# Seven products instead of eight in the second channel product too, in the wide chunks of a spectral filter with a token and channel MLP

## The chip, the cores and the metric

One Trainium2 chip, one of its cores. The metric is device time in microseconds of one execution. TensorE (PE) does the matrix products, with its weight loads (PEld) shown apart; VectorE (DVE), ScalarE (ACT) and GpSimd (POOL) do elementwise work; SyncE (SP) issues most transfers. Matrix results lie in PSUM, in eight banks of 128 x 512 f32; everything else is in SBUF.

## The reference, cut to what matters

```python
X = np.fft.rfft(x, axis=1)                       # x: (8, 3008, 256)
Yr = Xr @ w_r - Xi @ w_i + b_r                   # the same for Yi; both soft-thresholded
x = np.fft.irfft(Y, n=3008, axis=1)
h = np.maximum(xt @ w_tok1, 0.0) @ w_tok2        # xt: x with tokens last; d_tok = 256
u = x + h.transpose(0, 2, 1)
h2 = np.maximum(u @ w_ch1, 0.0) @ w_ch2          # 256 -> 1536 -> 256 channels
return u + h2
```

The change lies in the last product, `@ w_ch2`, for the batches 2 to 7.

## The kernel before, in words

The kernel first works through the spectra (TensorE, with VectorE, ScalarE and GpSimd beside it), interleaved with the channel MLP of batches 0 and 1. From 1133 us on, the channel MLP of batches 2 to 7 runs alone: this is `channel7`, the stage that the change rewrites. Its tokens come in 18 wide chunks, six for each pair of batches: one of 896 tokens, then five of 1024. `uf` holds a chunk's u: 128 channels on the partitions, two channel blocks t, tokens along the row. The hidden layer has 12 blocks of 128, taken as six pairs p; one chunk and one pair is called a step here (108 steps).

Every product is done to float32 accuracy in three matmuls (`mm3`, lines 196 to 198): operands are split into a rounded high part and a remainder, the low part, and high x high, high x low and low x high are summed in PSUM.

In a step, u is a 2 x 2 block matrix (two channel blocks by two halves of the tokens), and so is the pair's part of w_ch1. `first7` (L1018) does this product in Strassen's form (Winograd's variant): seven products of 128 x 128 by 128 x 512 in place of eight. The seven operands of u are made once a chunk (`sum_u` L991, `split_u7` L1004), those of the weights once for the kernel (`weigh`, during the last narrow chunk), and the four results are put together from PSUM and from copies of PSUM (`sn`) by ScalarE and VectorE; `rectify` (L1029) then makes the high part (ScalarE, L1032) and the low part (VectorE, L1033) of each of the four rectified blocks. `second7` (L1061) multiplies these blocks with w_ch2 as plain blocks: eight products a step, into four PSUM banks (`pos`) that collect over the six pairs. It runs one step behind `first7`. At the end of a chunk `finish7` adds u and stores.

Between the steps `make_u` (L841) makes the u of a coming chunk, one group of 376 or 470 tokens at a time: its matmuls are the `pu` rows of the profile, and its results are copied to `uf` by ScalarE (L867).

The order of the work: each engine runs its own queue in order. The order in a queue is not the order of the Python text alone: at build time a scheduler emits instructions by priority (text order) among those that it holds for ready. So what stands on each engine is read from the built kernel.

## Time and profile before

| | us |
|---|---|
| three timed runs | 2397.62, 2397.76, 2399.40; median 2397.76 |
| profiled execution, own time | 2399.55 |
| its span | 2397.8 |
| the stage of the wide chunks | from 1133.1 to the end |
| PE, DVE, ACT, POOL busy over the span | 98%, 59%, 48%, 11% |

POOL works only ahead of 1134 us; in the stage of the wide chunks it does nothing. The profile counts a matmul as busy from its start until its result has landed, and matmuls overlap; what one costs in a dense queue is the distance between two starts.

### The profile page before, as it was taken

The page shows a single profiled execution, that of the slowest core. Times are in us where ns is not written, and L with a number is a line of the kernel's source. Part 1 is how long each engine was busy: PE and PEld are TensorE (multiplying, and loading weights), DVE is VectorE, ACT ScalarE, POOL GpSimd, SP SyncE. Part 2 cuts the span into 40 slices and gives each one's busy share as a digit, 9 for nine tenths or more (in the row PEclk, how much of TensorE's full clock was granted, in tenths as well). Part 3 has the DMA queues.
Part 4 walks back from the last instruction along what each step waited for, and adds up shares of the span by engine and source line. Part 5 has one row for each costly group of instructions (what it writes and reads, how often), then busy time and mean ns, then how long its engine had stood idle before and what let it go on. Part 6 is the DMA issues. An engine that isn't in the chain of part 4 may idle for free.

```text
span 2397.8 us, 32249 instructions
## 1 busy us (share of the span) xinstructions
PE 2360.6 (98%) x12524; PEld 2063.7 (86%) x12524; DVE 1417.6 (59%) x2220; ACT 1143.3 (48%) x2033; POOL 252.7 (11%) x223
## 2 busy tenths in 40 slices
PE   8999999999999999999999999999999999999999
PEld 7778899999988888898988888898888889888887
DVE  7966766655646564555555555555555555555554
ACT  6754445544434443433444444444444444444543
POOL 0000332232323322330000000000000000000000
PEclk9999999999999999999999999999999999999999
DMA  8765467655555545433213112122311112222100
GB/s 217 237 222 158 152 205 241 198 167 181 176 181 169 185 149 171 141 128 126 64 60 91 57 49 61 37 81 60 91 57 38 52 57 82 60 86 60 40 1 36
DMA packets 149766, 277.06 MB, mean 116 GB/s; under 512 B 10933, under 2 KB 94477, under 8 KB 149613
## 3 DMA queue, kind: packets, MB, share of 16 engines
q1 hardware_dynamic: 115225, 208.40, 29.5%
q10 hardware_dynamic: 34388, 66.60, 8.2%
q8 instruction: 99, 1.62, 0.3%
q14 instruction: 54, 0.44, 0.1%
HBM read 177.57 MB, written 97.39 MB: 115 GB/s over the span
## 4 chain that ended last, share of the span: by engine, by line
PE 87%; DVE 5%; DMA 3%; ACT 1%; issue 1%; POOL 1%; SPq 1%; ACTq 0%; DVEq 0%; POOLq 0%
PE po L196 10%; PE po L197 10%; PE po L198 10%; PE pu L860 5%; PE sx L196 3%; PE sx L197 3%; PE sx L198 3%; PE px L482 2%; PE ph L196 2%; PE ph L197 2%; PE ph L198 2%; PE sw L196 2%; PE pm L198 2%; PE sw L197 2%; PE sw L198 2%; PE pm L196 2%
## 5 line engine op out<-in xcount | busy, mean ns | idle before, releaser
L196 PE MATMUL po<-hh,w2h 128*128 128x512 f32 (+3 forms) x1176 | 453.4, 386 | 1.2 <-DVE o L965 0.9
L197 PE MATMUL po<-hlo,w2h 128*128 128x512 f32 (+3 forms) x1176 | 449.3, 382 | 1.1 <-DVE hlo L899 1.1
L198 PE MATMUL po<-hh,w2l 128*128 128x512 f32 (+3 forms) x1176 | 449.1, 382 | 0.0
L1032 ACT ACTIVATE hh<-sn 128x512 fp32r<-128x512 f32 (+1 forms) x432 | 270.7, 627 | 86.5 <-DVE sn L1052 56.8
L1033 DVE SCALAR_TENSOR_TENSOR hlo<-sn,hh 128x512 fp32r<-128x512 f32 (+1 forms) x432 | 291.0, 674 | 10.0 <-ACT hh L1032 0.6
L197 PEld LDWEIGHTS po<-hlo,w2h 128*128 128x128 f32 x1176 | 221.2, 188 | 38.3 <-DVE hlo L899 2.2
L196 PEld LDWEIGHTS po<-hh,w2h 128*128 128x128 f32 x1176 | 221.2, 188 | 38.1 <-ACT xf L484 1.0
L198 PEld LDWEIGHTS po<-hh,w2l 128*128 128x128 f32 x1176 | 221.0, 188 | 38.0
L1041 DVE TENSOR_TENSOR sn<-sq,sn 128x512 f32<-128x512 f32 (+1 forms) x108 | 73.4, 680 | 290.1 <-PE sq L198 266.8
L1037 ACT COPY sn<-sx 128x512 f32<-128x512 f32 (+1 forms) x108 | 62.5, 579 | 341.4 <-PE sx L198 341.3
L149 DVE TENSOR_TENSOR xtl<-xf,xth 128x768 fp32r<-128x768 f32 x84 | 85.1, 1013 | 117.9 <-ACT xth L146 117.8
L196 PE MATMUL pm<-wmh,xth 128*128 128x256 f32 x504 | 146.2, 291 | 4.8 <-ACT xth L146 3.0
L899 DVE SCALAR_TENSOR_TENSOR hlo<-ph,hh 128x512 fp32r<-128x512 f32 (+3 forms) x156 | 98.7, 636 | 82.6 <-ACT hh L898 82.1
L867 ACT COPY uf<-pu 128x470 f32<-128x470 f32 (+15 forms) x152 | 60.5, 425 | 178.3 <-PE pu L860 177.5
L198 PE MATMUL pm<-wmh,xtl 128*128 128x256 f32 x504 | 142.6, 285 | 0.8 <-DVE xtl L149 0.8
L197 PE MATMUL pm<-wml,xth 128*128 128x256 f32 x504 | 142.4, 283 | 0.0
L860 PEld LDWEIGHTS pu<-g,b 96*128 96x128 f32 x1024 | 133.1, 194 | 3.5
L898 ACT ACTIVATE hh<-ph 128x512 fp32r<-128x512 f32 (+3 forms) x156 | 86.4, 556 | 103.1 <-PE ph L198 91.9
L860 PE MATMUL pu<-g,b 96*128 96x94 f32 x1024 | 131.3, 274 | 0.0
L149 POOL TENSOR_TENSOR yl<-z,yh 128x512 fp32r<-128x512 f32 x72 | 95.9, 1332 | 274.2 <-ACT yh L146 268.1
L196 PE MATMUL ph<-uh,w 128*128 128x512 f32 (+3 forms) x312 | 118.9, 382 | 3.6 <-DVE hlo L899 2.7
L197 PE MATMUL ph<-ul,w 128*128 128x512 f32 (+3 forms) x312 | 116.2, 373 | 0.0
(185 smaller groups left out, 5223.6 us busy)
## 6 DMA issues: line engine op xcount, KB each, us to landing
wt<-wt_d SPq DMA_DIRECT2D x28, 940.0 KB, 5.8
x<-in_x SPq DMA_DIRECT2D x39, 480.0 KB, 4.9
wt<-ws_d SPq DMA_DIRECT2D x36, 512.0 KB, 4.3
a<-a_d SPq DMA_DIRECT2D x36, 512.0 KB, 5.5
b_d<-bt ACTq DMA_DIRECT2D x36, 512.0 KB, 5.5
a_d<-a ACTq DMA_DIRECT2D x36, 480.0 KB, 4.0
wt<-wt_d SPq DMA_DIRECT2D x21, 752.0 KB, 5.2
b<-b_d SPq DMA_DIRECT2D x32, 480.0 KB, 6.5
```

The source lines that it names most:

```text
L149: lo_eng.tensor_tensor(out=lo, in0=src, in1=hi.bitcast(F32), op=ALU.subtract)
L196: PE.matmul(out, lhsT=wh, rhs=xh, start=start, stop=False, skip_group_check=more)
L197: PE.matmul(out, lhsT=wh, rhs=xl, start=False, stop=False, skip_group_check=more)
L198: PE.matmul(out, lhsT=wl, rhs=xh, start=False, stop=stop, skip_group_check=more)
L860: PE.matmul(pt[:, s * TOKS:(s + 1) * TOKS], lhsT=b2[:, s, cs], rhs=g2[:, 0 if s0 + s == 0 else 1], start=False, stop=s == k - 1)
L867: S.copy(out=ufs[m][:, ct, lo - at:hi - at], in_=pt[:, lo - c0:hi - c0])
L898: S.activation(out=hh, in_=pt, func=AF.Relu)
L899: V.scalar_tensor_tensor(out=hlo, in0=pt, scalar=0.0, in1=hh.bitcast(F32), op0=ALU.max, op1=ALU.subtract)
L1032: S.activation(out=hh, in_=t, func=AF.Relu)
L1033: V.scalar_tensor_tensor(out=hlo, in0=t, scalar=0.0, in1=hh.bitcast(F32), op0=ALU.max, op1=ALU.subtract)
L1037: S.copy(out=snap[0], in_=x)
L1041: V.tensor_tensor(out=snap[0], in0=q, in1=snap[0], op=ALU.add)
```

## The change

The second product gets the same seven-product scheme. The rectified block matrix (two hidden blocks by two token halves) is now what u is for the first product, and the pair's part of w_ch2 takes the role of the weights. New in the code:

- `weigh2` makes the weight operands of w_ch2, during the last narrow chunk beside `weigh`. Three operands of each set are kept apart (`ws`, `ws2`), and the fourth is written over the weight block that is no longer needed.
- `begin_pair` gives a step seven operands `op` (high and low side by side) in nine buffers; `high` makes the high parts on ScalarE. `lower` makes five low parts on GpSimd (b22, t1, t2, t4, t3), `above` two on VectorE (b11, b21).
- `step` writes a step of both products as one sequence: `one(new, i)` are the seven products of w_ch1 for the new step, `two(old, i)` the seven of w_ch2 for the step before. `snap` copies a PSUM bank to SBUF on ScalarE. t1, t2, t4 are sums on VectorE, t3 is one on GpSimd.
- Of the seven second products, five collect in PSUM over the six pairs (`total`); the products 3 and 4 each belong to one quarter of the output and are added to `uf` in every step (`taken`, VectorE). At a chunk's end the sums of the totals are added to `uf`: seven additions on VectorE, two on GpSimd.
- `first_u` and `rest_u` make the seven operands of u (seven splits and four sums a chunk, as before), with smaller buffers. `make_u` in this stage uses the banks x and y of the step in place of a bank of its own, and comes behind a step that `when` picks.

The diff, with weights and buffers that only change place left out:

```diff
 def make_u(g):
-            pt = bank("pu")
+            pt = wc["banks"]["xy"[ct]] if "banks" in wc else bank("pu")
...
+    def weigh2(q):
...
+        V.tensor_tensor(out=a.rearrange("m p t i c -> m (p t i c)"), in0=h.rearrange("m f c -> m (f c)").bitcast(F32), in1=l.rearrange("m f c -> m (f c)").bitcast(F32), op=ALU.add)
...
+        split(ws[:, :, :, 0], ws[:, :, :, 1], sf[:, :, :3], S, V)
+        split(h[:, 0::2, 128:], l[:, 0::2, 128:], s4, S, V)
...
+    FIRST = {1: ("x", "b11"), 2: ("y", "b21"), 3: ("w", "b22"), 4: ("x", "t4"), 5: ("w", "t1"), 6: ("x", "t2"), 7: ("x", "t3")}
+    SECOND = {1: "b11", 2: "b21", 3: "b22", 4: "t4", 5: "t1", 6: "t2", 7: "t3"}
...
     def channel7(ns):
...
+        total = {1: pair[0][:, 0], 5: pair[0][:, 1], 6: pair[1][:, 0], 7: pair[1][:, 1], 2: bank("po")}
+        banks = wc["banks"] = {k: bank("s" + k) for k in ("x", "w", "y")}
...
+        def begin_pair(n, p):
+            h = chunks[n][2] // 2
+            ops = {k: tail.tile([128, 2, CW], F32R, tag="op", name="op", bufs=9)[:, :, :h] for k in ("b11", "b22", "t1", "b21", "t2", "t4", "t3")}
+            return n, p, h, ops, {}
...
+        def above(out, in0, in1, op):
+            V.scalar_tensor_tensor(out=out, in0=in0, scalar=0.0, in1=in1, op0=MAX, op1=op)
...
+        def high(new, k, src=None):
+            S.activation(out=new[3][k][:, 0], in_=new[4][k] if src is None else src, func=AF.Relu if k in ("b11", "b21") else AF.Copy)
+
+        def lower(new, k, eng=G):
+            add(new[3][k][:, 1], new[4][k], new[3][k][:, 0].bitcast(F32), eng, SUB)
+
+        def taken(old, i, q):
+            out = quarters(old[0])[q]
+            add(out, banks["y"][:, :old[2]], out)
+
+        def step(new, old, last=False):
...
+            if new:
+                one(new, 1)
+                v["b11"] = snap(new, "x")
+                one(new, 5)
+                v["b22"] = snap(new, "w")
+            if old:
+                two(old, 1)
...
+            if new:
+                one(new, 6)
+                v["x2"] = snap(new, "x")
+                one(new, 2)
+                add(v["b11"], b["y"][:, :h], v["b11"])
+                high(new, "b11")
+                one(new, 3)
+                add(v["x2"], b["w"][:, :h], v["x2"])
+                S.activation(out=v["x2"], in_=v["x2"], func=AF.Relu)
+                one(new, 7)
+                add(v["b22"], b["x"][:, :h], v["b22"])
+                S.activation(out=v["b22"], in_=v["b22"], func=AF.Relu)
+                high(new, "b22")
+            if old:
+                two(old, 3)
+                taken(old, 3, 1)
+            if new:
+                sums(new, "t1", "t2", "t4", "t3")
+                above(v["t1"], v["b11"], v["x2"], SUB)
+                add(v["t2"], v["b22"], v["t1"])
+                high(new, "t1")
+            if old:
+                two(old, 5)
+            if new:
+                one(new, 4)
+                high(new, "b21", b["x"][:, :h])
+                above(v["t4"], b["x"][:, :h], v["t2"], SUB)
+                above(new[3]["b21"][:, 1], b["x"][:, :h], new[3]["b21"][:, 0].bitcast(F32), SUB)
+                high(new, "t2")
+                high(new, "t4")
+                lower(new, "t1")
+                add(v["t3"], v["b22"], v["x2"], G, SUB)
+                above(new[3]["b11"][:, 1], v["b11"], new[3]["b11"][:, 0].bitcast(F32), SUB)
+                high(new, "t3")
+                for k in ("b22", "t2", "t4", "t3"):
+                    lower(new, k)
...
+            if old:
+                two(old, 2)
...
+                two(old, 6)
...
+                two(old, 4)
+                taken(old, 4, 2)
+                two(old, 7)
+                if ends:
+                    add(fin, L[7], fin)
+                    for t in (u21, u22):
+                        add(t, fin, t, V if last else G)
+                    store(old[0])
...
+            for p in range(half):
+                new = begin_pair(n, p)
+                step(new, old)
+                old = new
+                if n < ns[-1] and p == half - 2:
+                    first_u(n + 1)
+                if n < ns[-1] and p == half - 1:
+                    rest_u(n + 1)
+                if (n, p) in when:
+                    make_u(when[n, p])
+                    load_group(when[n, p] + 1)
+        step(None, old, True)
```

The built order shows what this puts on the engines in a step. ScalarE before, one step of two 512-token halves: `sn` are the copies from PSUM (L1037, L1039, L1043, L1049), `hh7` the four high parts.

```order
L1037 COPY sn_15515<-sx_15511 128x512 [waits PE_49]
L1039 COPY sn_15516<-sw_15512 128x512 [waits PE_49]
L1043 COPY sn_15517<-sx_15511 128x512 [waits PE_49,Activation_49]
L1032 ACTIVATE hh7_15535<-sn_15515 128x512 [waits DVE_49]
L1049 COPY sn_15518<-sz_15514 128x512 [waits PE_49,Activation_49]
L1032 ACTIVATE hh7_15543<-sn_15517 128x512 [waits DVE_49]
L1032 ACTIVATE hh7_15556<-sn_15518 128x512 [waits DVE_49]
L1032 ACTIVATE hh7_15560<-sn_15516 128x512 [waits DVE_49]
```

Eight instructions, and none waits for GpSimd. The same engine now, from the second copy of bank x in a step to the first copy of the next step: `sn_17093` is x2, `sn_17085` b22, and `op_17070` to `op_17076` are, by number, the operands b11, b22, t1, b21, t2, t4, t3; the `ts` are the sums t1, t2, t4, t3.

```order
L1108 COPY sn_17093<-sx_10834 128x512 [waits PE_49]
L1112 ACTIVATE op_17070<-sn_17080 128x512 [waits DVE_49]
L1147 ACTIVATE sn_17093<-sn_17093 128x512 [waits DVE_49]
L1150 ACTIVATE sn_17085<-sn_17085 128x512 [waits DVE_49]
L1112 ACTIVATE op_17071<-sn_17085 128x512 [waits Activation_49]
L1112 ACTIVATE op_17072<-ts_17115 128x512 [waits DVE_49]
L1112 ACTIVATE op_17073<-sx_10834 128x512 [waits PE_49]
L1112 ACTIVATE op_17074<-ts_17116 128x512 [waits DVE_49]
L1112 ACTIVATE op_17075<-ts_17117 128x512 [waits DVE_49]
L1112 ACTIVATE op_17076<-ts_17118 128x512 [waits Pool_49]
L1108 COPY sn_17164<-sx_10834 128x512 [waits PE_49]
```

The step has twelve instructions on this engine in place of eight; the high part of t3 waits for GpSimd, and the next step's first copy of bank x stands behind it in the queue.

GpSimd, which had nothing in this stage, at the end of one chunk and in the first step after it: the two `uf` rows are the chunk's closing additions, `op_17071` is the low part of b22, `op_17072` that of t1, `ts_17118` is the sum t3.

```order
L1101 TENSOR_TENSOR uf_15484<-t_16992,uf_15484 128x512 [waits DMAHW2_49,DMAHW1_49,DVE_49]
L1101 TENSOR_TENSOR uf_15484<-t_16992,uf_15484 128x512
L1101 TENSOR_TENSOR op_17071<-sn_17085,op_17071 128x512 [waits PE_49,Activation_49]
L1101 TENSOR_TENSOR op_17072<-ts_17115,op_17072 128x512 [waits PE_49,Activation_49]
L1101 TENSOR_TENSOR ts_17118<-sn_17085,sn_17093 128x512 [waits Pool_49]
L1101 TENSOR_TENSOR op_17074<-ts_17116,op_17074 128x512 [waits PE_49,Activation_49]
L1101 TENSOR_TENSOR op_17075<-ts_17117,op_17075 128x512 [waits PE_49,Activation_49]
L1101 TENSOR_TENSOR op_17076<-ts_17118,op_17076 128x512 [waits PE_49,Activation_49]
```

Six instructions a step have moved here or are new; the sum t3 is third, behind the low parts of b22 and t1.

VectorE now, one step, from the sum b11 to the low part of b21: `sn<-sy`, `sn<-sw` and `sn<-sx` are the sums b11, x2 and b22, `op_17154` and `op_17157` the low parts of b11 and b21, `uf` the two `taken`, `ts_17199`, `ts_17200` and `ts_17201` are t1, t2 and t4.

```order
L1101 TENSOR_TENSOR sn_17164<-sy_10836,sn_17164 128x512 [waits Activation_49]
L1104 SCALAR_TENSOR_TENSOR op_17154<-sn_17164,op_17154 128x512 [waits Activation_49]
L1101 TENSOR_TENSOR sn_17177<-sw_10835,sn_17177 128x512 [waits PE_49,Activation_49,Pool_49]
L1101 TENSOR_TENSOR sn_17169<-sx_10834,sn_17169 128x512 [waits PE_49]
L1101 TENSOR_TENSOR uf_16115<-sy_10836,uf_16115 128x512 [waits PE_49]
L1104 SCALAR_TENSOR_TENSOR ts_17199<-sn_17164,sn_17177 128x512 [waits Activation_49]
L1101 TENSOR_TENSOR ts_17200<-sn_17169,ts_17199 128x512 [waits DVE_49,Activation_49,Pool_49]
L1101 TENSOR_TENSOR uf_16115<-sy_10836,uf_16115 128x512 [waits PE_49]
L1104 SCALAR_TENSOR_TENSOR ts_17201<-sx_10834,ts_17200 128x512 [waits DVE_49,Activation_49,Pool_49]
L1104 SCALAR_TENSOR_TENSOR op_17157<-sx_10834,op_17157 128x512
```

Ten instructions where there were eight (four sums and four low parts); those without a PSUM operand (`sx`, `sw`, `sy`) are three: the low part of b11, t1 and t2.

More of the change, by code (lines that the diff above doesn't have):

```diff
@@ L988, in weigh @@
         ws = wc["ws"][:, 2 * q:2 * q + 2]
[L989 to L997 removed]
+        split(ws[:, :, :, 0], ws[:, :, :, 1], sf[:, :, :3], S, V)
+        h, l = (w1[:, k, 0, cols].rearrange("m (p i f) -> m p i f", p=2, i=2)[:, :, 1] for k in range(2))
@@ new lines, in quarters, with divide, spare @@
+    def quarters(n):
+        h = chunks[n][2] // 2
+        uf = us[n][0]
+        return [uf[:, t, k * h:(k + 1) * h] for t in range(2) for k in range(2)]
+    def divide(n, k, src):
+        ub = us[n][1][k] = wc["seven"].tile([128, 2, CW], F32R, tag="ub", name="ub", bufs=8)[:, :, :chunks[n][2] // 2]
+        split(ub[:, 0], ub[:, 1], src, S, V)
+    def spare(n):
+        if "tail" in wc:
+            return wc["tail"].tile([128, CW], F32, tag="t", name="t", bufs=3)[:, :chunks[n][2] // 2]
+        if "spare" not in wc:
+            wc["spare"] = [wc["wk2"].tile([128, 2, CW], F32, tag=k, name="t")[:, i, :chunks[n][2] // 2] for k in ("uh", "ul") for i in range(2)]
+        return wc["spare"].pop()
@@ L998, in sum_u, with first_u, rest_u @@
+    def first_u(n):
+        us[n] = ufs.pop(n), {}
+        b11, b12, b21, b22 = quarters(n)
+        divide(n, "b11", b11)
+        t1 = spare(n)
         V.tensor_tensor(out=t1, in0=b12, in1=b11, op=ALU.subtract)
-        V.tensor_tensor(out=t2, in0=b22, in1=t1, op=ALU.subtract)
+        divide(n, "t1", t1)
+    def rest_u(n):
+        b11, b12, b21, b22 = quarters(n)
+        t2, t3, t4_ = (spare(n) for _ in range(3))
         V.tensor_tensor(out=t3, in0=b22, in1=b12, op=ALU.subtract)
+        V.tensor_tensor(out=t2, in0=t3, in1=b11, op=ALU.add)
@@ L1001, in sum_u @@
         V.tensor_tensor(out=t4_, in0=b21, in1=t2, op=ALU.subtract)
-        us[n] = uf, (b11, t1, b21, t2, b22, t4_, t3), []
-    def split_u7(n, i):
-        h = chunks[n][2] // 2
-        _, srcs, done = us[n]
-        ub = wc["seven"].tile([128, 2, CW], F32R, name="ub", bufs=9)
-        split(ub[:, 0, :h], ub[:, 1, :h], srcs[i], S, V)
-        done.append(ub)
-    def left(p, i):
-        w1 = wc["w1"]
-        if i < 4:
-            return [wc["ws"][:, p, i, k] for k in range(2)]
-        f, ct = {4: (0, 0), 5: (0, 1), 6: (1, 1)}[i]
-        return [w1[:, k, ct, (2 * p + f) * 128:(2 * p + f + 1) * 128] for k in range(2)]
@@ new lines, in tile_kernel, with left, load_group @@
+    MADE = {5: 0, 6: 1, 7: 2}
+    KEPT = {1: (0, 0), 2: (0, 1), 3: (1, 0), 4: (1, 1)}
+    def left(layer, p, i):
+        if i in MADE:
+            return [wc["ws" if layer == 1 else "ws2"][:, p, MADE[i], k] for k in range(2)]
+        row, t = KEPT[i]
+        if layer == 1:
+            return [wc["w1"][:, k, t, (2 * p + row) * 128:(2 * p + row + 1) * 128] for k in range(2)]
+        return [wc[name][:, 2 * p + t, row * 128:(row + 1) * 128] for name in ("w2h", "w2l")]
+    def load_group(g):
+        if g < len(groups):
+            if gts[groups[g][0]] is None or groups[g][0] != groups[g - 1][0]:
+                fetch_g(groups[g][0])
+            load_wt2(g)
+            load_b2(g)
@@ new lines, in one, with two @@
+        def one(new, i):
+            n, p, h, _, _ = new
+            k, src = FIRST[i]
+            ub = us[n][1][src]
+            more = i in (3, 4, 6, 7)
+            mm3(banks[k][:, :h], *left(1, p, i), ub[:, 0], ub[:, 1], not more, True, more)
+        def two(old, i):
+            n, p, h, ops, _ = old
+            op = ops[SECOND[i]]
+            if i in total:
+                mm3(total[i][:, :h], *left(2, p, i), op[:, 0], op[:, 1], p == 0, p == half - 1)
+            else:
+                mm3(banks["y"][:, :h], *left(2, p, i), op[:, 0], op[:, 1], True, True)
@@ new lines, in store @@
+        def store(n):
+            u, at, cw = chunks[n]
+            h = cw // 2
+            uf = us[n][0]
+            for k in range(2):
+                for b, bi in enumerate(UNITS[u]):
+                    lo, hi = max(at + k * h, b * N), min(at + (k + 1) * h, (b + 1) * N)
+                    if lo < hi:
+                        DMA.dma_start(out=outv[bi][:, :, lo - b * N:hi - b * N], in_=uf[:, :, lo - at:hi - at])
+        when = {}
+        for m in ns[1:]:
+            mine = needs[m]
+            if m == ns[1]:
+                spots = [(ns[0], p) for p in range(len(mine))]
+            else:
+                spots = [(m - 2, half - len(mine) + 1 + i) for i in range(len(mine) - 1)] + [(m - 1, 3)]
+            for spot, g in zip(spots, mine):
+                assert spot not in when
+                when[spot] = g
@@ L1094, in channel7 @@
+        old = None
         for n in ns:
[L1095 to L1096 removed]
             for p in range(half):
[L1098 to L1120 removed]
```

177 lines of the change are left out of this document (63 added, 114 removed).

## The prediction

> **What bounds the kernel now.** I read the page first, then the table of stretches, the waits within the stage of the wide chunks, and the timeline of a step. The busy line of the page:
>
> ```profile
> PE 2360.6 (98%) x12524; PEld 2063.7 (86%) x12524; DVE 1417.6 (59%) x2220; ACT 1143.3 (48%) x2033; POOL 252.7 (11%) x223
> ```
>
> A stretch of the last narrow chunk and one within the stage (PE, PEld, DVE, ACT, POOL busy with counts, then granted clock, DMA share, GB/s):
>
> ```profile
> 1080.00:1134.00 54.00, 54.00 (x262) 45.82 (x262) 31.55 (x49) 20.41 (x37) 2.71 (x2) 1.00 0.42 130
> ...
> 1400.00:1600.00 200.00, 200.00 (x974) 172.12 (x973) 112.13 (x175) 95.10 (x175) 0.00 (x0) 1.00 0.22 68
> ```
>
> PE has no gap in the stage, at full clock; DVE is busy 56% of it, ACT 48%, POOL not at all. The longest waits there are those of the other engines for PE; the only one of PE's own side is a weight load that waited 0.3 us at most, behind running matmuls:
>
> ```profile
> ACT sn L1037 <- PE sx L198: 341.3, 107, 4.1
> DVE sn L1041 <- PE sq L198: 266.8, 83, 9.0
> ...
> PEld sx L196 <- ACT sn L1043: 3.3, 13, 0.3
> ```
>
> So the stage lasts as long as its matmuls take. What one takes is the distance of starts in a dense stretch of the timeline: first and last of 26 matmuls of 512 columns, and of ten of 448.
>
> ```profile
> 2370.13 0.39 PE L196 MATMUL sw<-ub,ws 128*128 128x512 f32 x1
> ...
> 2375.79 0.39 PE L197 MATMUL po<-hlo,w2h 128*128 128x512 f32 x1
> ```
>
> ```profile
> 1133.12 0.36 PE L196 MATMUL sx<-ub,w 128*128 128x448 f32 x1
> ...
> 1134.94 0.37 PE L196 MATMUL sz<-ub,w 128*128 128x448 f32 x1
> ```
>
> 5.66 us over 25 gives 0.2264 us; 1.82 over 9 gives 0.202 us. The 0.39 us of a row is the time until its result has landed. A product is three matmuls, 0.68 us in the queue, and its result stands 2 x 0.2264 + 0.39 = 0.84 us after its start. A step of 15 products (45 matmuls) costs 10.19 us.
>
> **The change part by part.** *Removed.* One product a step: 90 steps of 512 columns and 18 of 448. 270 x 0.2264 + 54 x 0.202 = 61.1 + 10.9 = 72.0 us. All of it lies on the path. A step would then need 42 x 0.2264 = 9.51 us of PE.
>
> *What the engines must do in it.* These are the nearest rows for the step's new operations: a sum with a PSUM operand, a two-operand VectorE instruction from SBUF alone, the high part, the copy from PSUM, and POOL's low part (taken from the spectra, where POOL works).
>
> ```profile
> L1033 DVE SCALAR_TENSOR_TENSOR hlo<-sn,hh 128x512 fp32r<-128x512 f32 x360 | 246.4, 684 | 7.6
> ...
> L1051 DVE TENSOR_TENSOR sn<-sx,sn 128x512 f32<-128x512 f32 x90 | 62.2, 691 | 5.6 <-PE sx L198 0.4
> ```
>
> ```profile
> L1032 ACT ACTIVATE hh<-sn 128x512 fp32r<-128x512 f32 x360 | 228.7, 635 | 73.9 <-DVE sn L1052 49.5 <-DVE sn L1051 24.4
> ...
> L1037 ACT COPY sn<-sx 128x512 f32<-128x512 f32 x90 | 52.9, 588 | 291.0 <-PE sx L198 291.0
> ```
>
> ```profile
> L149 POOL TENSOR_TENSOR yl<-z,yh 128x512 fp32r<-128x512 f32 x72 | 95.9, 1332 | 274.2 <-ACT yh L146 268.1 <-issue 5.8
> ```
>
> Back to back, instructions start closer together than they last: VectorE 0.60 us apart, ACT 0.48, POOL 1.25.
>
> ```profile
> 1307.79 0.69 DVE L999 TENSOR_TENSOR t<-uf,t 128x512 f32<-128x512 f32 x1 [0.32 <-ACT uf L867]
> 1308.39 0.69 DVE L1000 TENSOR_TENSOR t<-uf 128x512 f32<-128x512 f32 x1
> ```
>
> ```profile
> 1313.13 0.59 ACT L1043 COPY sn<-sx 128x512 f32<-128x512 f32 x1 [0.77 <-PE sx L198]
> 1313.61 0.63 ACT L1032 ACTIVATE hh<-sn 128x512 fp32r<-128x512 f32 x1
> ```
>
> ```profile
> 252.48 1.29 POOL L149 TENSOR_TENSOR y<-z,y 128x512 fp32r<-128x512 f32 x1 [3.34 <-ACT y L146]
> 253.73 0.74 POOL L485 TENSOR_TENSOR xf<-xf 128x256 f32<-128x256 f32 x1
> ```
>
> By these, a step asks of VectorE 10 x 0.60 = 6.0 us, of ACT about 12 x 0.5 = 6, of POOL 6 x 1.25 = 7.5. None of them alone fills 9.51 us. But POOL and VectorE are not independent: a VectorE instruction with both operands in SBUF (L519) beside POOL, one with a PSUM operand (L511), and POOL's own (min/median/max in ns):
>
> ```profile
> L519 DVE TENSOR_TENSOR z<-z x84: 676/693/1782, 246.4 to 1081.5; 128x512 f32<-128x512 f32 x84
> ```
>
> ```profile
> L511 DVE TENSOR_TENSOR z<-pm,bias x96: 675/687/694, 31.4 to 1078.7; 128x512 f32<-128x512 f32 x96
> ```
>
> ```profile
> L149 POOL TENSOR_TENSOR yl<-z,yh x72: 1264/1292/1872, 470.5 to 1083.9; 128x512 fp32r<-128x512 f32 x72
> ```
>
> One such meeting in the timeline; the VectorE instruction ends 0.55 us after POOL's has ended, as if it had only then begun to stream:
>
> ```profile
> 313.59 1.78 DVE L519 TENSOR_TENSOR z<-z 128x512 f32<-128x512 f32 x1
> ```
>
> ```profile
> 313.40 1.42 POOL L149 TENSOR_TENSOR wt<-aw,wt 128x512 fp32r<-128x512 f32 x1 [2.98 <-ACT wt L146]
> ```
>
> So one shuts the other out: up to 1.1 us for VectorE, up to 0.6 us for POOL; a PSUM operand spares VectorE (694 at most). A step has three VectorE instructions of the shut-out kind (t1, t2, low part of b11): 3 x 0.60 + 7.5 = 9.3 us of a common resource.
>
> Here the Trainium skill speaks against the change: "SBUF — State Buffer", section "SBUF: two separate sides", has VectorE's second port pair in common with GpSimd, held whole by whichever instruction starts first, and fully blocking the other. These rows agree; by the rule at its worst, each of the three POOL instructions of the loop below would wait for a VectorE one, and the sum would end near 2480 (68 steps x 1.35 more than the 0.3 counted there); by the rows' usual case it is the sum below.
>
> *The loop.* A step's products on bank x are added up with copies between: product 1, copy, product 6, copy, product 7, sum b22. In the order of ACT, the next step's first copy of bank x stands behind the high part of t3, which waits for POOL's third instruction, which waits for b22. That closes a ring through four engines. The handing-over times, with two rows each:
>
> ```profile
> 1310.61 0.39 PE L198 MATMUL sx<-ub,w 128*128 128x512 f32 x1
> ...
> 1311.09 0.59 ACT L1037 COPY sn<-sx 128x512 f32<-128x512 f32 x1 [2.90 <-PE sx L198]
> ```
>
> ```profile
> 604.41 0.62 ACT L146 CAST yh<-z 128x512 fp32r<-128x512 f32 x1 [0.79 <-DVE z L519]
> ...
> 605.11 1.28 POOL L149 TENSOR_TENSOR yl<-z,yh 128x512 fp32r<-128x512 f32 x1 [4.22 <-ACT yh L146]
> ```
>
> ```profile
> 1305.39 0.69 DVE L998 TENSOR_TENSOR t<-uf 128x512 f32<-128x512 f32 x1 [1.95 <-ACT uf L867]
> ...
> 1306.12 0.62 ACT L146 CAST ub<-t 128x512 fp32r<-128x512 f32 x1 [0.32 <-DVE t L998]
> ```
>
> PE to ACT 0.09, ACT to POOL 0.08, DVE to ACT 0.04 us (taken for POOL to ACT and ACT to ACT too). After a wait PE loses more than the handing-over; the copy at 421.00 released this matmul, and the next came 0.34 in place of 0.23 us behind it:
>
> ```profile
> 421.00 0.58 ACT L271 COPY a<-p 120x512 f32<-120x512 f32 x1 [2.49 <-DMA a_d<-a]
> ...
> 421.63 0.50 PE L196 MATMUL p<-xh,f1r 120*128 120x512 f32 x1 [0.38 <-ACT a L271]
> ...
> 421.97 0.39 PE L197 MATMUL p<-xl,f1r 120*128 120x512 f32 x1
> ```
>
> Once round, from the start of the sum b22: sum 0.69, rectify 0.04 + 0.64, high part 0.04 + 0.64, to POOL 0.08: 2.13. POOL's low parts of b22 and t1 and the sum t3: 1.29 + 2 x 1.25, and 0.3 since t2 on VectorE (1.8 to 2.5) meets the first: 6.2. High part of t3 to the start of the copy 0.04 + 0.5, copy 0.59, to PE 0.05: 7.4. Product 6 after a wait (0.34 + 0.23 + 0.39 = 0.96), 0.09, copy 0.59, 0.05: 9.1. Product 7, 0.84 to 0.96 and up to 0.2 for a product that PE has begun meanwhile, 0.09: 10.0 to 10.3. I take 10.15 us. That is PE's 9.51 plus 0.64 of standing still, and about what a step costs now (10.19).
>
> Where a `make_u` lies in the step, PE has over 4 us more to do, ahead of product 1, and the ring is covered. Their number, from the grouped rows (four such matmuls for a group):
>
> ```profile
> L196 PE MATMUL pu<-wt,gh 128*128 128x470 f32 (+1 forms) x158 | 59.4, 376 | 0.0
> ```
>
> That is 40 groups with the first ones of the stage, so 68 of 108 steps have none: 57 wide x 0.64 + 11 narrow x 0.56 (by width) = +43 us.
>
> *Ends of chunks.* Seven splits and four sums of the next chunk are as before, and `make_u` lies on that place. New are nine closing additions. The two on POOL take 2.5 us; POOL's spare time in a round is 10.15 - 7.5 - 0.9 for the meetings = 1.75, so the next step is late by 0.75, and VectorE's seven add perhaps 0.15: 0.9 x 17 = +15 us. Below, 0 (all hidden), above, 2.5 + 7 x 0.60 = 6.7 each.
>
> *Ahead of the stage.* `weigh2` adds VectorE work three times: sums over 1024, four of 256, remainders of 768 and 256, by 0.60 us for 512 columns an estimated 1.2 + 1.2 + 1.2 = 3.6 us each, to a stretch in which VectorE is idle 22 of 54 us: nearly hidden, +2, with 0 and 11 as ends. First step, without second products to fill in: +1.
>
> *The end.* The last seven products wait for POOL's last low parts, 1.6 us by the same walk, and three additions follow the last product where two did: +3 with the stores.
>
> Sum: 2399.55 - 72.0 + 43 + 15 + 2 + 1 + 3 = 2391.6 for the profiled execution's own time (span 2397.8, 1.75 around it). That execution lay 1.8 above the median of the three runs, 2397.76. So **2389.8** for the median, 8 below.
>
> **The rivals.** *PE stays the bound.* If POOL meets nothing and the ring comes to 9.5, each step stalls 0.1 at most: 7 in place of 43, ends 4 in place of 15: 2343. For it: each engine's own load is under 80% of 9.51. Against: the ring's parts are measured rows, and would have to be 0.6 us shorter. Chance 0.22.
>
> *POOL and VectorE shut each other out oftener, and the kernel gets slower.* The mechanism lies between the low part of b22 and the sum t3: if one more of POOL's three instructions there waits 0.55 us for t2, a split or the low part of b11, the ring is 10.7, and 68 x 0.55 = 37 more: 2427; with two, 2464. It decides from 10.15 + (2402.6 - 2389.8)/68 = 10.34 us for a round on; so 0.2 us is all that parts it from my forecast. For it: 9.3 of 10.15 us of that resource are asked for, and the splits of the next chunk come on top. Against: the order puts only t1 and t2 near that place, and t1 falls into POOL's idle time. Chance 0.28.
>
> *The forecast*, ring 10.15 +- 0.2: 2376 to 2404, chance 0.45. That the change doesn't take the products away is no rival: the built order has 324 matmuls fewer. 0.05 is left for what I don't see.
>
> **How the numbers follow.** A measurement of this kernel tells about 0.2%, 4.8 us, from no change: faster is under 2393.0, slower over 2402.6. The forecast's 0.45 divides into 0.28, 0.13 and 0.04; with the rivals and the rest: faster 0.28 + 0.22 + 0.02 = 0.52, same 0.13 + 0.01 = 0.14, slower 0.04 + 0.28 + 0.02 = 0.34. The range goes from the first rival's 2343 to the second's 2427.
>
> **What would show it.** Right: within the stage PE idle about 0.6 us in each step without `make_u`, put down to ACT's copies of bank x; ACT's wait ahead of the high part of t3 ended by POOL; POOL busy about 75% of the stage, its instructions at 1.3 to 1.5 us. Wrong: a PE without gaps (first rival), POOL's mean over 1.6 us or t2 and the low part of b11 near 1.2 us (second), or PE waiting first for something that isn't in the ring, such as bank x behind the low part of b21, or gaps of several us at chunk ends.

## The result and the profile after

| | us |
|---|---|
| before, four timed runs | 2390.80 to 2399.40; median 2397.69 |
| after, four timed runs | 2546.06 to 2551.68; median 2548.61 |
| ratio, with its 95% interval | 1.0636 (1.0612 to 1.0660) |
| profiled execution after, own time and span | 2546.06, 2544.3 |

The changed kernel is 6.4% slower: 151 us over the kernel before, 159 us over the 2389.8 that was forecast, and beyond the range. The page's line of busy times, and the same two stretches as before (PE, PEld, DVE, ACT, POOL, then clock, DMA share, GB/s):

```profile
PE 2374.4 (93%) x12200; PEld 1988.2 (78%) x12200; DVE 1831.6 (72%) x2551; ACT 1398.1 (55%) x2492; POOL 1216.3 (48%) x905
```

```profile
1080.00:1134.00 54.00, 53.95 (x267) 45.88 (x265) 37.60 (x64) 25.55 (x49) 1.99 (x2) 1.00 0.42 130
1400.00:1600.00 200.00, 182.28 (x823) 141.29 (x823) 158.31 (x199) 123.28 (x223) 135.56 (x95) 1.00 0.19 57
```

The 324 matmuls are gone and the granted clock is full in this stretch, but PE, which had no gap in it, now stands still for 18 us of 200. The stretch ahead of the stage is as full as before. The granted clock isn't the cause: it falls to 0.83 to 0.94 between 1160 and 1250 us, but from 1250 to 1600 us it is 1.00, and a step takes 13.25 us there, against 11.32 in the run with three memsets below, also at 1.00. No engine is saturated: VectorE is at 79%, GpSimd at 68%. So something waits for something that is not throughput. Within the stage, the waits (engine and line, for whom; total us, times, longest):

```profile
ACT op L1112 <- DVE ts L1104: 107.2, 147, 2.8
...
ACT op L1112 <- POOL ts L1101: 74.2, 68, 1.9
...
PEld sx L196 <- DVE op L1104: 61.3, 55, 2.7
PEld sx L196 <- ACT sn L1108: 56.5, 129, 1.5
```

PE's weight loads (PEld) wait longest for bank x behind VectorE's low part of b21 (L1104), a little more than for the copy (L1108) on which the forecast had put it. What VectorE's instructions last there (min/median/max in ns), with two SBUF operands (the first five: t2, low part of b11, two kinds of split, one of the sums of u) and with one PSUM operand (the last two):

```profile
L1101 DVE TENSOR_TENSOR ts<-sn,ts x107: 621/1372/1795, 1144.4 to 2527.3; 128x512 f32<-128x512 f32 x90, 128x448 f32<-128x448 f32 x17
```

```profile
L1104 DVE SCALAR_TENSOR_TENSOR op<-sn,op x107: 614/691/1786, 1141.2 to 2525.3; 128x512 fp32r<-128x512 f32 x90, 128x448 fp32r<-128x448 f32 x17
```

```profile
L149 DVE TENSOR_TENSOR ub<-t,ub x68: 624/1603/1834, 1190.4 to 2463.7; 128x512 fp32r<-128x512 f32 x60, 128x448 fp32r<-128x448 f32 x8
L149 DVE TENSOR_TENSOR ub<-uf,ub x51: 616/1767/1789, 1188.8 to 2459.1; 128x512 fp32r<-128x512 f32 x45, 128x448 fp32r<-128x448 f32 x6
...
L1038 DVE TENSOR_TENSOR t<-uf x17: 1073/1775/1780, 1163.0 to 2437.7; 128x512 f32<-128x512 f32 x15, 128x448 f32<-128x448 f32 x2
```

```profile
L1104 DVE SCALAR_TENSOR_TENSOR ts<-sx,ts x107: 607/678/694, 1145.4 to 2529.0; 128x512 f32<-128x512 f32 x90, 128x448 f32<-128x448 f32 x17
...
L1101 DVE TENSOR_TENSOR sn<-sw,sn x107: 609/681/694, 1141.7 to 2524.1; 128x512 f32<-128x512 f32 x90, 128x448 f32<-128x448 f32 x17
```

Those with a PSUM operand never pass 694 ns; the others are held up by as much as 1.1 us, the splits most of the time. One place in the timeline shows what follows from it. VectorE, GpSimd and PE:

```profile
1696.25 1.78 DVE L1104 SCALAR_TENSOR_TENSOR op<-sn,op 128x512 fp32r<-128x512 f32 x1
1697.96 1.77 DVE L1101 TENSOR_TENSOR ts<-sn,ts 128x512 f32<-128x512 f32 x1
1699.87 0.69 DVE L1104 SCALAR_TENSOR_TENSOR ts<-sx,ts 128x512 f32<-128x512 f32 x1
1700.47 0.68 DVE L1104 SCALAR_TENSOR_TENSOR op<-sx,op 128x512 fp32r<-128x512 f32 x1
```

```profile
1696.03 1.46 POOL L1101 TENSOR_TENSOR op<-sn,op 128x512 fp32r<-128x512 f32 x1 [0.25 <-ACT op L1112]
1697.44 1.74 POOL L1101 TENSOR_TENSOR op<-ts,op 128x512 fp32r<-128x512 f32 x1
1699.15 1.72 POOL L1101 TENSOR_TENSOR ts<-sn 128x512 f32<-128x512 f32 x1
```

```profile
1698.58 0.39 PE L198 MATMUL sw<-ub,ws 128*128 128x512 f32 x1
1701.21 0.50 PE L196 MATMUL sx<-ub,w 128*128 128x512 f32 x1 [2.24 <-DVE op L1104]
```

GpSimd and VectorE go in turns, the low part of b22, that of b11, the low part of t1, t2: each instruction waits for the other engine's. Behind t2 stand t4 and the low part of b21, which is the last to read bank x; so PE gets the bank late and loses 2.24 us. GpSimd's result isn't in this path; VectorE's own queue is late.

How long a step takes, from the starts of the sums b11 (`sn<-sy`; first and last of the 107 rows found):

```profile
1139.92 0.62 DVE L1101 TENSOR_TENSOR sn<-sy,sn 128x448 f32<-128x448 f32 x1 [5.90 <-ACT sn L1108]
...
2523.36 0.69 DVE L1101 TENSOR_TENSOR sn<-sy,sn 128x512 f32<-128x512 f32 x1 [3.85 <-PE sy L198]
```

1383.4 us in 106 distances is 13.05 on the mean: 11.90 for the 67 without `make_u`, where the forecast had 10.15 and the kernel before, counted in the same way by its sums `sn<-sq`, has 10.09, and 15.02 for the 39 with it (before 14.21).

One step stands out, the fifth of the first wide chunk: 25.79 us, where the fifth steps of the other two chunks of 896 tokens take 11.75 and 11.77. The third `weigh2`, and the third `weigh` but for its first sum, don't run during the last narrow chunk; they run here. VectorE makes their sums, and PE waits for the weights:

```profile
1179.24 0.76 DVE L989 TENSOR_TENSOR sf<-a 128x256 f32<-128x256 f32 x2 [0.99 <-PE sy L198]
...
1180.84 1.22 DVE L1000 TENSOR_TENSOR a<-w2h,w2l 128x1024 f32<-128x1024 f32 x1
...
1186.51 0.95 DVE L149 TENSOR_TENSOR ws<-sf,ws 128x768 fp32r<-128x768 f32 x1
```

```profile
1181.26 0.47 PE L196 MATMUL sw<-ub,ws 128*128 128x448 f32 x1 [2.05 <-ACT ws L146]
```

The kernel before, which needs `weigh` alone, had finished it by 1109.5 us.

### The profile page after: what moved, and what is told of

Same layout as the page of the kernel before. It is cut to its first block, busy times and chain, and to the rows that moved or that the text cites. A ratio compares the mean times of both kernels' runs of the same rounds, so it can differ in the third digit from the quotient of the medians.

```text
span 2544.3 us, 33504 instructions
## 1 busy us (share of the span) xinstructions
PE 2374.4 (93%) x12200; PEld 1988.2 (78%) x12200; DVE 1831.6 (72%) x2551; ACT 1398.1 (55%) x2492; POOL 1216.3 (48%) x905
## 4 chain that ended last, share of the span: by engine, by line
PE 44%; DVE 17%; POOL 15%; issue 14%; ACT 4%; DMA 3%; SPq 1%; DVEq 0%; ACTq 0%; POOLq 0%
POOL op L1101 11%; DVE sn L1101 3%; PE po L197 3%; PE po L196 3%; PE po L198 3%; POOL ts L1101 3%; PE px L482 2%; DVE ts L1101 2%; PE ph L196 2%; PE pm L198 2%; PE pm L196 2%; PE ph L198 2%; PE ph L197 2%; PE pm L197 2%; DVE ts L1104 2%
## 5 line engine op out<-in xcount | busy, mean ns | idle before, releaser
L1101 POOL TENSOR_TENSOR op<-ts,op 128x512 fp32r<-128x512 f32 (+1 forms) x432 | 618.1, 1451 | 0.0
L1112 ACT ACTIVATE op<-ts 128x512 fp32r<-128x512 f32 (+1 forms) x432 | 264.9, 619 | 257.8 <-DVE ts L1104 107.2
L1101 POOL TENSOR_TENSOR op<-sn,op 128x512 fp32r<-128x512 f32 (+1 forms) x108 | 166.4, 1541 | 493.7 <-ACT op L1112 439.2
L1112 ACT ACTIVATE op<-sn 128x512 fp32r<-128x512 f32 (+1 forms) x216 | 134.6, 623 | 80.2 <-DVE sn L1101 77.2
L1101 DVE TENSOR_TENSOR sn<-sy,sn 128x512 f32<-128x512 f32 (+1 forms) x108 | 73.1, 676 | 139.0 <-ACT sn L1108 84.6
L1108 ACT COPY sn<-sx 128x512 f32<-128x512 f32 (+1 forms) x216 | 123.6, 572 | 60.2 <-PE sx L198 58.2
L1101 DVE TENSOR_TENSOR uf<-sy,uf 128x512 f32<-128x512 f32 (+1 forms) x216 | 144.8, 671 | 6.5 <-PE sy L198 6.4
L1101 POOL TENSOR_TENSOR ts<-sn 128x512 f32<-128x512 f32 (+1 forms) x108 | 148.9, 1379 | 0.0
L1101 DVE TENSOR_TENSOR ts<-sn,ts 128x512 f32<-128x512 f32 (+1 forms) x108 | 126.5, 1172 | 8.4 <-ACT op L1112 0.5
L196 PE MATMUL po<-op,ws 128*128 128x512 f32 (+1 forms) x324 | 128.9, 398 | 3.4 <-ACT op L1112 1.5
L197 PE MATMUL po<-op,ws 128*128 128x512 f32 (+1 forms) x324 | 128.3, 396 | 3.9 <-POOL op L1101 3.9
L1104 DVE SCALAR_TENSOR_TENSOR op<-sn,op 128x512 fp32r<-128x512 f32 (+1 forms) x108 | 107.5, 995 | 31.1 <-ACT op L1112 31.1
L198 PE MATMUL po<-op,ws 128*128 128x512 f32 (+1 forms) x324 | 127.4, 393 | 0.0
```

What stands on the lines that cost most here:

```text
L196: PE.matmul(out, lhsT=wh, rhs=xh, start=start, stop=False, skip_group_check=more)
L197: PE.matmul(out, lhsT=wh, rhs=xl, start=False, stop=False, skip_group_check=more)
L198: PE.matmul(out, lhsT=wl, rhs=xh, start=False, stop=stop, skip_group_check=more)
L1101: eng.tensor_tensor(out=out, in0=in0, in1=in1, op=op)
L1104: V.scalar_tensor_tensor(out=out, in0=in0, scalar=0.0, in1=in1, op0=MAX, op1=op)
L1108: S.copy(out=t, in_=banks[k][:, :new[2]])
```

## The experiments

Theory A says that GpSimd and VectorE shut each other out, and that VectorE's late queue is the loss. Theory B says that VectorE's queue is too long at a chunk's end, whatever GpSimd does. Rival 2 of the prediction says that the ring through GpSimd gets longer. Each time stands beside runs of the kernel before on the same chip, whose medians were 2393 to 2395; step means are given without and with `make_u`. The code cuts show only the lines that matter.

**GpSimd reads nothing in the steps.** (The two closing additions of a chunk stay on it.)

```diff
+        def fill(out):
+            for i in range(2):
+                G.memset(out, 0.0)
...
-            add(new[3][k][:, 1], new[4][k], new[3][k][:, 0].bitcast(F32), eng, SUB)
+            fill(new[3][k][:, 1].bitcast(F32))
...
-                add(v["t3"], v["b22"], v["x2"], G, SUB)
+                fill(v["t3"])
```

> Changed kernel, with each of GpSimd's six instructions in a step replaced by two memsets on its output; the low parts of b22, t1, t2, t4, t3 and the sum t3 become constants, so the output is not the reference's. GpSimd's order and waits stay, and it reads nothing from SBUF. Theory A (GpSimd and VectorE's two-SBUF-operand instructions shut each other out, and the splits and sums of the next chunk at a chunk's end do so most): the 161 us over 10.15 (13.9 with make_u) a step go as far as memsets don't shut VectorE out: t2, the low part of b11 and the splits back to 0.70 us, time about 2548 - 161 = 2387. Theory B (VectorE's queue is simply too long at a chunk's end, whatever GpSimd does): the stalls at chunk ends stay, about 2548. If memsets shut VectorE out as well, both give 2548 and VectorE's durations stay at 1.2 us and more; that tells nothing between A and B.

2366.3 us, ratio to before 0.989 (0.987 to 0.991), 1.1% under the kernel before. Steps 9.81 and 13.87. Theory B is out as an account of the whole loss: VectorE has the same 2551 instructions as in the changed kernel.

**No GpSimd work in the steps.**

```diff
+            low = ops["b11" if i == 1 else "b21"][:, 1]
...
-                mm3(total[i][:, :h], *left(2, p, i), op[:, 0], op[:, 1], p == 0, p == half - 1)
+                mm3(total[i][:, :h], *left(2, p, i), op[:, 0], low, p == 0, p == half - 1)
...
-                lower(new, "t1")
-                add(v["t3"], v["b22"], v["x2"], G, SUB)
...
-                high(new, "t3")
-                for k in ("b22", "t2", "t4", "t3"):
-                    lower(new, k)
+                high(new, "t3", v["b22"])
```

> Changed kernel without GpSimd's six instructions in a step: the second products 3, 5, 4, 6, 7 take the low part of b21 for their own, product 7 the high part of b22, so the output is not the reference's. PE, VectorE and ScalarE have the instructions they had. Theory A with the ring through GpSimd (0.64 us a step): both go, PE has no gaps beyond small ones, 2548 - 161 - 43 = 2344. Theory B: only the ring goes, 2548 - 43 = 2505.

2361.3, ratio 0.987 (0.985 to 0.989); steps 9.86 and 13.86. The same 200 us of the stage:

```profile
1400.00:1600.00 200.00, 199.83 (x959) 165.65 (x958) 144.26 (x231) 136.72 (x254) 7.65 (x6) 1.00 0.22 68
```

PE is full again. The memsets cost only 5 us more: GpSimd's presence in the order and the waits for it cost next to nothing at their length.

**GpSimd as long as in the change, without reading.** The two memsets left GpSimd shorter (2 x 0.53 us). Two runs make up for it: 512 + 512 + 352 columns, and three times 512.

```diff
-            for i in range(2):
-                G.memset(out, 0.0)
+            for w in (out.shape[-1], out.shape[-1], 352):
+                G.memset(out[:, :w], 0.0)
```

```diff
-            for i in range(2):
+            for i in range(3):
                 G.memset(out, 0.0)
```

> The run with memsets again (2366), but with three memsets for each of GpSimd's six instructions, two of 512 columns and one of 352, together about 1.45 us: what these instructions took on the mean in the changed kernel, blocked time included. The low parts of b22, t1, t2, t4, t3 and the sum t3 are constants again. GpSimd's own time and the ring are then as in the changed kernel; what is missing is that VectorE is shut out. If the loss is GpSimd's length (rival 2 as the prediction put it: a longer ring): close to the changed kernel, 2500 or more. If it is what VectorE loses: the ring of three times 1.45 makes plain steps about 10.4 and no more, 67 x 0.6 = 40 over 2366: about 2405.

> Three memsets of 512 columns for each of GpSimd's six instructions (low parts of b22, t1, t2, t4, t3 and the sum t3 are constants): 3 x 0.47 = 1.41 us each in the queue, close to the 1.45 us that GpSimd's instructions last in the changed kernel, and VectorE is not shut out. If GpSimd's own blocked time matters as the ring has it: 3 x 0.14 = 0.42 us more a ring than the run with 1.27, at most 67 x 0.42 = 28 more: 2377 to 2405. If GpSimd's length were the cause of the loss: well over 2450.

GpSimd's memsets in the first of them stand 0.47, 0.47 and 0.33 us apart, so what takes an instruction's place is 1.27 us in the queue, less than the 1.45 expected; in the second run it is 3 x 0.47 = 1.41.

```profile
1695.00 0.53 POOL L1116 MEMSET op<- 128x512 f32 x1 [0.40 <-ACT op L1112]
1695.47 0.53 POOL L1116 MEMSET ts<- 128x512 f32 x1
1695.94 0.39 POOL L1116 MEMSET op<- 128x352 f32 x1
1696.27 0.53 POOL L1116 MEMSET ts<- 128x512 f32 x1
```

2376.8 and 2375.7 us, ratios 0.992 (0.990 to 0.995) and 0.992 (0.988 to 0.996); steps 10.11 and 13.71, 9.95 and 13.97. With three memsets of 512 columns GpSimd is busier than in the changed kernel, and VectorE's splits aren't held up any more, nor is t2 (696 ns at most):

```profile
1400.00:1600.00 200.00, 199.26 (x958) 166.01 (x956) 143.20 (x230) 135.10 (x251) 158.93 (x329) 1.00 0.22 69
```

```profile
L149 DVE TENSOR_TENSOR ub<-t,ub x68: 610/682/694, 1184.0 to 2296.5; 128x512 fp32r<-128x512 f32 x60, 128x448 fp32r<-128x448 f32 x8
L149 DVE TENSOR_TENSOR ub<-uf,ub x51: 612/682/694, 1182.9 to 2295.3; 128x512 fp32r<-128x512 f32 x45, 128x448 fp32r<-128x448 f32 x6
```

Only t1 still meets GpSimd in the steps after a chunk's end, where GpSimd goes on reading for its two closing additions:

```profile
L1104 DVE SCALAR_TENSOR_TENSOR ts<-sn x107: 611/680/1604, 1140.1 to 2351.4; 128x512 f32<-128x512 f32 x90, 128x448 f32<-128x448 f32 x17
```

A GpSimd that is busy for 79% of the time costs 14 us against the run without its work, as long as it doesn't read SBUF in the steps. So its length explains 14 of the 187 us at most. (The scheduler placed VectorE's and PE's instructions somewhat differently in these two runs.)

**GpSimd's work done, and read by nobody.** As the run without GpSimd's work, with its six instructions left in.

```diff
+                lower(new, "t1")
+                add(v["t3"], v["b22"], v["x2"], G, SUB)
...
                 high(new, "t3", v["b22"])
+                for k in ("b22", "t2", "t4", "t3"):
+                    lower(new, k)
```

> Changed kernel with all of GpSimd's instructions in their places, but nobody reads their results: the second products take the low part of b21 (b11 for product 1) for their own low part, and the high part of t3 is made from b22, so the output is not the reference's. The ring holds no instruction of GpSimd; VectorE is shut out as before. If what VectorE loses is nearly all of the loss: 2361 + 130 to 170, 2490 to 2530. If it counted only through the ring: 2361 to 2400.

2528.1, ratio 1.055 (1.052 to 1.058); steps 11.51 and 15.19, t2 and the splits as long as in the changed kernel:

```profile
L1102 DVE TENSOR_TENSOR ts<-sn,ts x107: 607/1368/1795, 1145.4 to 2508.4; 128x512 f32<-128x512 f32 x90, 128x448 f32<-128x448 f32 x17
```

```profile
1400.00:1600.00 200.00, 184.07 (x817) 144.73 (x816) 159.25 (x196) 118.96 (x216) 138.46 (x95) 0.97 0.19 57
```

This settles it. The two runs have the same order on PE, VectorE and ScalarE, and against 2361.3, 167 us come from GpSimd's instructions whose results nobody uses. No wait that the profile lists in the stage ends with GpSimd, so buffers that GpSimd holds aren't the way either; VectorE's longer instructions are what is left. Waiting for the results is the other 2548.6 - 2528.1 = 20 us, with a few us open (the mean granted clock is 0.984 here, 0.989 in the changed kernel).

By the place of a step in its chunk, the work that nobody reads costs, against the run without it, 0.4 us in the third step and 0.6 in the fourth, but 1.4 to 2.5 in each of the four around a chunk's end (fifth, sixth, first, second): 8.2 of 9.2 us a chunk. Waits for GpSimd show in the third step: 10.75 us in the changed kernel, 9.88 here, 9.51 without GpSimd's work.

**Splits and sums left out.**

```diff
+        if "tail" in wc and chunks[n][2] == chunks[n - 1][2]:
+            us[n] = ufs.pop(n), us[n - 1][1]
+            return
```

> Changed kernel without the four sums and seven splits of the next chunk at the 12 of 17 chunk ends where both chunks have one width; the operands of the chunk before are used again, so the output is not the reference's. If the loss at chunk ends (161 us over 17 ends, 9.5 us each) comes from these eleven VectorE instructions and what they meet, by theory A or B: 12 x 9.5 = 114 less, 2434. If it comes from the nine closing additions, two of them on GpSimd (theory C): at most 12 x 1 less, 2535 or more.

2499.5, ratio 1.045 (1.042 to 1.048): 49 less, between the two expectations. So at 12 of 17 ends the eleven instructions cost 4.1 us each time, 70 us if all 17 are alike; the rest of the loss hangs on the steps' own instructions.

**Only t3 moved, and only the closing additions moved.**

```diff
-                add(v["t3"], v["b22"], v["x2"], G, SUB)
+                add(v["t3"], v["b22"], v["x2"], V, SUB)
```

```diff
-                        add(t, fin, t, V if last else G)
+                        add(t, fin, t, V)
```

> Changed kernel, all of it computed, with the sum t3 alone moved from GpSimd to VectorE. The ring from b22 to the high part of t3 then holds no instruction of GpSimd. If the ring sets the plain steps (10.4 to 10.6 us, as the prediction has it): they come to about 9.6, and the rest loses a little less too: 67 x 0.9 = 60 less, about 2490. If the load on what VectorE and GpSimd share sets them: 0.60 in place of 1.25 us, 0.65 a step, at most 70 less, with VectorE's durations hardly shorter. If neither does (VectorE's queue is what counts): one instruction more a step on VectorE, 2548 to 2600.

> Changed kernel, all of it computed, with the two closing additions of a chunk that GpSimd did (u21 and u22) on VectorE. The prediction charged these two with 0.75 us a chunk's end. By that: 17 x 0.75 = 13 less, and 1.2 us more on VectorE that may eat it: 2535 to 2555. If they hold up GpSimd's low part of b22 in the first steps of a chunk by their whole length: 17 x 2.5 = 43 less, 2505.

2514.5, ratio 1.050 (1.048 to 1.052), and 2566.0, ratio 1.072 (1.070 to 1.073). Taking t3 off GpSimd gives 34, by a shorter ring or one meeting less (this run can't part them). With the two closing additions on VectorE the time grows by 17, and neither expectation is met. That run says little about the two additions themselves: the scheduler also placed PE's products differently, and PE then waits for GpSimd's low parts, which it hardly does in the changed kernel (3.5 us, three times):

```profile
PE po L197 <- POOL op L1101: 64.8, 64, 1.9
```

**Looking for a version that keeps the gain.** Six kernels, all computing everything, share the work otherwise. In the first everything of GpSimd's goes to VectorE (t3 and the closing additions too).

```diff
-        def lower(new, k, eng=G):
+        def lower(new, k, eng=V):
```

> Changed kernel, all of it computed, with everything that GpSimd did in the stage moved to VectorE: 16 instructions a step and 20 at a chunk's end. No instruction can be shut out any more, and VectorE's should last 0.69 us throughout. What is left is VectorE's own queue: around a chunk's end (three steps) 68 instructions of 0.608 us, the spacing seen in the run with the ring on VectorE, are 41.3 us, against 34.5 us that the same three steps take without GpSimd's work; 17 x 6.8 = 116 over 2361, and some 0.5 to 1 us for each of the two plain steps: 2490 to 2510. If the shut-out were the whole of the loss and VectorE's load none of it: about 2361.

2518.2, ratio 1.052 (1.050 to 1.054). VectorE is then 91% busy in the 200 us, so its queue is taken for the bound:

```profile
1400.00:1600.00 200.00, 191.04 (x842) 145.13 (x841) 181.77 (x300) 125.19 (x226) 0.00 (x0) 0.98 0.19 57
```

In the next, b22's and t1's low parts and t3 go to VectorE; in the one after it t3 also stands ahead of t4.

```diff
-                lower(new, "t1")
-                add(v["t3"], v["b22"], v["x2"], G, SUB)
+                lower(new, "t1", V)
+                add(v["t3"], v["b22"], v["x2"], V, SUB)
...
+                lower(new, "b22", V)
```

> Changed kernel, all of it computed, with the low parts of b22 and t1 and the sum t3 moved from GpSimd to VectorE. VectorE then has 13 instructions a step and 20 a chunk's end, 13 x 0.60 + 20 x 0.60 / 6 = 9.8 us a step; GpSimd three, 3.75 us, and none in the ring. Theory A: what only one of the two can use is asked for less (six of 0.60, three of 1.25 and eleven a chunk of 0.60: 8.5 us a step in place of 10.4), and a step comes near VectorE's 9.8 (make_u steps 14.3): 68 x 2.1 + 39 x 0.7 = 170 less, about 2380. Theory B: VectorE's queue at chunk ends has more in it, the loss stays or grows: 2540 to 2580.

> The kernel with the low parts of b22 and t1 and the sum t3 on VectorE (2559), all of it computed, with t3 put ahead of t4 and both ahead of the low parts in VectorE's and ScalarE's order, so that the next step's copy of bank x stands 1 to 2 us less far behind. Plain steps there took 10.14 to 10.18; with the ring shorter they should come to 9.3 to 9.6, chunk ends stay bound by VectorE's 46 instructions in two steps (15.2 + 12.7 us): about 35 x 0.7 = 25 less, 2535. If plain steps stay at 10.15, something else than the ring holds them.

2559.4, ratio 1.069 (1.068 to 1.071), and 2565.2, ratio 1.071 (1.069 to 1.073). Both hopes failed: less is asked of what the two share, but in the first of them the first two steps of a chunk of 1024 tokens take 15.0 and 12.7 us. VectorE starts 17.7 and 14.8 instructions in them, 10.6 and 8.9 us at 0.60 us each, so their number alone doesn't explain it; what does is open. Moving t3 ahead brought the third step no gain (10.2, then 10.9 us).

```diff
-        split(ub[:, 0], ub[:, 1], src, S, V)
+        split(ub[:, 0], ub[:, 1], src, S, G if k in ('b22', 't3', 't4') and "tail" in wc else V)
...
-                    add(u11, fin, u11)
+                    add(u11, fin, u11, V if last else G)
```

> The kernel with the new order, all of it computed, and besides the work at a chunk's end taken off VectorE: the low parts of three of the seven operands of u and two more closing additions on GpSimd, and the three later sums of u made a step earlier. VectorE then has 52 instructions in the three steps at a chunk's end, 52 x 0.608 = 31.6 us, under the 34.5 that PE needs for them; GpSimd has 16, 20 us; what both share is asked for 26 x 0.60 + 20 = 36 us in these three steps and 7.4 in a plain one. If loads on VectorE and on the shared part are what holds the chunk ends, this comes near the kernel without GpSimd's work (2361), with part of the shut-out left: 2380 to 2420, about 2400. If it is something else (the closing additions, or the order in which the operands of u come), it stays over 2500.

2575.4, ratio 1.075 (1.074 to 1.077), the slowest of all, though by its loads it should have been near 2400. Its timeline shows one reason, VectorE and then PE:

```profile
1482.44 1.78 DVE L1103 TENSOR_TENSOR op<-sn,op 128x512 fp32r<-128x512 f32 x1
1484.14 1.76 DVE L1103 TENSOR_TENSOR op<-ts,op 128x512 fp32r<-128x512 f32 x1
1485.82 0.68 DVE L1103 TENSOR_TENSOR uf<-sy,uf 128x512 f32<-128x512 f32 x1
```

```profile
1486.55 0.50 PE L196 MATMUL sy<-ub,w 128*128 128x512 f32 x1 [1.89 <-DVE uf L1103]
```

The sum that frees bank y stands behind two low parts that are shut out for 1.1 us each, and PE waits for the bank. In the next run these low parts come behind that sum.

```diff
                 taken(old, 4, 2)
+            if new:
+                lower(new, "b22", V)
+                lower(new, "t1", V)
```

> As the kernel that took 2575 (t2, t3, t4 lows on GpSimd, three of the seven low parts of u on GpSimd, sums of u a step earlier), all of it computed, with two changes: the low parts of b22 and t1 stand on VectorE behind the sum of bank y into uf, which frees the bank that PE's product 2 waits for (1.1 to 1.9 us in each plain step there), and the closing additions to u11 and u12 are back on VectorE (there VectorE, GpSimd, VectorE waited for one another in turn at a chunk's end). If those two waits are what held it, plain steps fall from 10.8 to 9.5 and the chunk ends (14.6 + 12.5 over two steps) by 3 us: 70 steps x 1 and 17 x 3 = 120 less, about 2455; if the shut-out of VectorE's low parts by GpSimd's three (1.35 us a step) holds the steps wherever they stand, plain steps stay near 10.5 and the time over 2530.

> As the run beside it, all of it computed, with the low part of t2 on VectorE too: 14 instructions a step on VectorE, two on GpSimd. If the shut-out counts more than VectorE's queue: 1.25 us less of GpSimd and one meeting less, up to 0.5 us a step, 50 us faster than the run beside it. If VectorE's queue counts more: 0.6 us a step slower, up to 65 us.

2482.5, ratio 1.038 (1.036 to 1.039), and 2486.5, ratio 1.039 (1.037 to 1.041): the same within the noise. Putting what frees a bank ahead of what nobody is waiting for yet is worth 93 us, together with GpSimd's own low parts placed later and two closing additions taken back to VectorE; no run parts the three. Steps without `make_u` fall from 12.66 to 11.22, and the third step of a chunk of 1024 tokens to 9.21 (9.43 without GpSimd's work). The rest stays around the chunk ends. It is the best version that computes everything, and still 3.8% behind the kernel before. The only runs faster than before are those in which GpSimd doesn't read SBUF in the steps, and they don't compute the reference's output.

## Why the prediction was wrong, point by point

- **72 us of matmuls removed.** They are gone, and without the shut-out in the steps the time is 2361 to 2377 against 2393 to 2395. So 18 to 32 of the 72 are gained; the forecast, with a ring through GpSimd and chunk ends, had left 8.
- **The loop, 10.15 us a step.** This is the step that failed, in the term "0.3 since t2 meets the first". That charged the meeting to GpSimd's side of the ring alone. VectorE's side, up to 1.1 us for each meeting, was quoted in the prediction's own row (L519, 1782 at most) and charged nothing, because t2 was not in the ring. But t4 and the low part of b21 stand behind t2 on VectorE and free bank x. Steps without `make_u` took 11.90, and 9.95 with three memsets: 67 x (11.90 - 9.95) = 131 us. The ring itself fits in the third step of a chunk, 10.75 us, against 9.88 where nobody reads GpSimd's results; that memsets give 9.95 and 10.11 is no proof of it, since PE is busy for 199.26 of 200 us there.
- **With `make_u` the ring is covered.** It is, the shut-out isn't: 15.02 against 13.97, 39 x 1.05 = 41. Together 172 us, which is 2548 against 2376; what follows on splits and on the fifth step is part of it.
- **Ends of chunks, 15 us.** The wrong step here was "as before" for splits and sums. They were measured at 0.69 us in a stage in which GpSimd slept; beside it the splits' medians are 1.60 and 1.77, and about 70 us of the loss hang on splits and sums, by the run that leaves them out at 12 ends. The nine closing additions, for which the 15 were, cost little by themselves: all of them stand in the run without GpSimd's work in the steps, which takes 2361.
- **Ahead of the stage.** PE is busy 53.95 of the 54 us there, but a third of the weights' work doesn't lie there: it had slipped into the fifth step of the first wide chunk. That step is 14.0 us longer than its like in the changed kernel, 11.7 without GpSimd's work and 10.1 with three memsets; the forecast had 2, with 11 as its upper end.
- **The end.** From the last sum b11 to the end of the span it is 20.9 us, 17.9 before; the +3 fits.
- **Rival 1.** 2343 is not reached even without GpSimd's work: 2361. About 10 of the 18 us between are that fifth step; the rest no run separates.
- **Rival 2** had the sign and the cause, at 0.28, but the wrong path. It priced 0.55 us of GpSimd's in the ring, 2427 to 2464. Waiting for GpSimd was worth about 20 us, and VectorE's lateness 167. Its first sign (GpSimd's mean over 1.6 us) stayed out, at 1.45; its second came true, with means of 1.21 for t2 and 1.02 for the low part of b11 (512 columns):

```profile
L1101 DVE TENSOR_TENSOR ts<-sn,ts 128x512 f32<-128x512 f32 x90 | 108.9, 1211 | 6.6 <-ACT op L1112 0.5
L1104 DVE SCALAR_TENSOR_TENSOR op<-sn,op 128x512 fp32r<-128x512 f32 x90 | 91.9, 1021 | 26.5 <-ACT op L1112 26.5
L149 DVE TENSOR_TENSOR ub<-t,ub 128x512 fp32r<-128x512 f32 x60 | 81.2, 1374 | 27.4 <-ACT ub L146 22.1 <-PE sx L198 5.3
...
L149 DVE TENSOR_TENSOR ub<-uf,ub 128x512 fp32r<-128x512 f32 x45 | 71.7, 1615 | 3.5 <-ACT ub L146 3.5
```

These four rows alone lose 90 x 0.52 + 90 x 0.33 + 60 x 0.69 + 45 x 0.92 = 159 us of VectorE's time over 0.69 an instruction.

- **The signs.** Three signs for "right" came out or nearly so, though the forecast was wrong: ACT's waits for GpSimd's t3 (74.2 us), GpSimd's instructions at 1.45 us, GpSimd busy for 68%. The sign that told was the one named last under "wrong", PE waiting for bank x behind the low part of b21; it stood there without a price.

The Trainium skill ("SBUF — State Buffer", section "SBUF: two separate sides") has a two-operand SBUF instruction of VectorE and a GpSimd instruction that reads SBUF exclude each other for a whole instruction, and was cited as speaking against the change, near 2480 at worst. The runs agree with the rule on both halves: reads shut VectorE out, memsets don't (694 ns at most in the splits). The "worst" counted only GpSimd's waits, and 2549 lies beyond it.
